# Attention into a two-layer expert on one Trainium2 core: fewer loads of x, three of seven low weight parts from DRAM, two sets of weight sums, the expert's load queue in written order

## The chip, the cores and the metric

The kernel runs on one core of a Trainium2 chip. It is one launch, and the metric is the device time of that launch in microseconds (us). The core has five engines that run side by side and meet at semaphores: TensorE (PE) multiplies into PSUM, VectorE (DVE) and ScalarE (ACT) read PSUM and SBUF, GpSimd (POOL) works on SBUF alone, and SyncE (SP) issues nearly all transfers here. Each engine takes its instructions strictly in the order in which they stand in its queue.

## The reference, cut to what matters

```
scores = q k^T / 8 + bias          # 4 batches x 8 heads x 576 x 576, heads of 64
attn   = exp(scores - max) / (sum + 1e-9)
x      = attn v, heads side by side           # 2304 tokens x 512
h = x @ w_in                                  # 512 -> 2048
g = h where h >= 1, 0 where h <= -1, else (h + 1)**2 / 4
out = g @ w_out                               # 2048 -> 512, float32
```

The bias is a small two-layer network of the distance of two positions.

## The kernel before

Every float32 operand of a product is split into a high part (a rounded copy) and a low part (the value minus its high part), and a product is three matmuls: high by high, high by low, low by high.

The program has three parts. The bias network comes first (to 72 us) and goes to DRAM. Attention follows (to about 324 us): 16 units of one batch and two heads each. Each unit's result is stored to `xT` in DRAM as values that are not yet divided, in a high and a low half, and the reciprocals of the sums of exponentials go to `rT`. The expert is the rest, over three blocks of 768 tokens (`TB`), each cut into two halves of 384 (`TH`).

Loading x for a block is eight loads (`load_x`), each of one row group k of 128 and one half j of the tokens: two transfers bring the two heads' rows, and several more bring the reciprocals, each spread over 64 partitions. The reciprocals' row in `rT` has the first 512 of both heads ahead of the last 64 of both, so a load is cut at 512 too. DVE then adds the two halves (L393) and multiplies by the reciprocal (L394).

Block 0 (324 to 453 us) multiplies plainly, in 32 steps `m` (16 slices of 128 rows f of the hidden layer, two halves). The same steps bring in the 14 weight slices of each layer that are still missing: `job(m, 0)` loads raw values, ACT and DVE put them in order, POOL makes the low part (L143), and the second layer's slices, once split, are stored to `w2d` (`job(m - 2, 6)`). The steps also prepare x of block 1.

Blocks 1 and 2 (from 453 us) share one loop with 16 groups g, eight in each block. A group is two slices f of the hidden layer by both halves, and by Winograd's form of Strassen's scheme it takes seven products instead of eight, steps `s_` 0 to 6; `t` counts steps through all groups. Steps 0, 2 and 5 multiply by a quarter of the first layer's weights as it is; steps 1, 3, 4 and 6 multiply by a sum of quarters. There are four such sums in four tiles `S_`, which DVE forms (L816, `sum_s`) one group ahead: sums 0 to 2 of group g + 1 at steps 1 to 3 of group g, and the last sum of g at its step 1. For each step the high part is made on ACT four steps ahead (L825, `high_w`) and the low part three steps ahead (L835, `low_w`), on DVE for step 1 and on POOL for the other six. So in each group POOL makes six low parts of weights and four low parts `gl` of the activations (L921).

The result of each step lands in one of two PSUM banks (`h_bank`), taken in turn. DVE combines it (L928) with what earlier steps left; until it has, PE can't begin the step after next. Four results of a group pass on: ACT squares (L913, L914), DVE clamps (L919), ACT makes `gh` (L920), POOL makes `gl`. Between the products, `chunks` runs the second layer's matmuls on the activations of the group before, 12 chunks in a group. The second layer's weights come back from `w2d` (L947).

Block 2's x is prepared inside the loop of block 1 (`make_x`): a table says at which step each load is issued and after how many steps DVE adds and multiplies; DVE forms four further matrices of differences (L768, `combine_x`), and `part_x` makes the high part on ACT (L774) and the low part on POOL (L775).

What sets the order: on PE, ACT, DVE and POOL the order of this part is that of the written program (`keep`). SP's queue was not held so: a scheduler placed the transfers.

Of the kernel before, what the change touches and what calls it, by code (L numbers as in the profile page):

```python
# [62 lines left out]
def attn_cpb_moe_kernel(ctx, tc, qk, vL, cb, win, wout, lw, ident, ii, out):  # L63
# [12 lines left out]
    rT = [[dram.tile([2 * S], F32, name=f"rT{p}_{b}") for b in range(B)] for p in range(NP)]  # L76
# [35 lines left out]
    def weight_ahead(f, o, rp):  # L112
# [32 lines left out]
        def store():  # L145
            if o:
                nc.sync.dma_start(out=w2d[f], in_=both[f].bitcast(F32))
# [4 lines left out]
    go = [False]  # L152

# [211 lines left out]
    def load_x(blk, k, j, home="x"):  # L365

        src = xT[k][blk // TB][:, :, TH * j : TH * j + TH].rearrange("(s d) i c -> d s i c", s=2)
# [10 lines left out]
        for i in range(2):  # L378
            nc.sync.dma_start(out=r[D * i : D * i + D], in_=src[:, :, i])
        c0 = blk + TH * j  # L380
        c1 = c0
        while c1 < c0 + TH:
            t = c1 % S
            e = min(c0 + TH, c1 - t + (512 if t < 512 else S))
            for i in range(2):
                at = 512 * i + t if t < 512 else 1024 + D * i + t - 512
                row = rT[k][c1 // S][at : at + e - c1].unsqueeze(0)
                nc.sync.dma_start(out=rr[D * i : D * i + D, c1 - c0 : e - c0], in_=row.to_broadcast((D, e - c1)))
            c1 = e
        return r, rr  # L390

    def scale_x(r, rr, out):
        keep(nc.vector.tensor_tensor(out=r[:, 0], in0=r[:, 0], in1=r[:, 1], op=ALU.add))  # L393
        keep(nc.vector.tensor_tensor(out=out, in0=r[:, 0], in1=rr, op=ALU.mult))  # L394
# [20 lines left out]
    with ExitStack() as ph:  # L415
# [39 lines left out]
        def unit(n):  # L455
# [124 lines left out]
            def store(half):  # L580
# [83 lines left out]
    with ExitStack() as ph:  # L664
# [12 lines left out]
        pinned = [False]  # L677

# [21 lines left out]
        def chunks(n_):  # L700
            for _ in range(n_):
# [12 lines left out]
                if last:  # L714
                    o = gp.tile([P, DM], F32, tag="o", name=f"o{blk}_{at_}", bufs=CFG["ob"])
                    r = blk + P * at_
                    if blk == 2 * TB and not made and len(prev) == 1 and t == TH // P - 1:
# [4 lines left out]
                        nc.sync.dma_start(out=out[r : r + P, h_:], in_=o[:, h_:])  # L722
                    else:
# [4 lines left out]
                        nc.sync.dma_start(out=out[r : r + P, :], in_=o)  # L728
                prev[0][-1] += 1
                if t == TH // P - 1:  # L730
                    prev.pop(0)

# [22 lines left out]
        def fill_x(blk, q):  # L755
            k, j, o, i = NEXT[q]
            r = load_x(blk, k, j, "x" if q % 2 else "y")

            def scale():
                stage[o, i] = room_b(q)  # L760
                scale_x(*r, stage[o, i])

            return scale
# [7 lines left out]
        def part_x(blk, o, k):  # L771
            h, l = xo[blk][o][k]
            x = stage[o, k]
            keep(nc.scalar.copy(h, x))  # L774
            keep(nc.gpsimd.tensor_tensor(out=l, in0=x, in1=h.bitcast(F32), op=ALU.subtract))  # L775
# [33 lines left out]
        def sum_s(g, which):  # L809
            if g >= 2 * NG2:  # L810
                return
            f = 2 * (g % NG2)
            (a11, a12), (a21, a22) = [[full[0, f + i][:, c : c + 2 * P] for c in (0, 2 * P)] for i in range(2)]
            for i in which:
                x, y, op = ((a21, a22, ALU.add), (S_[0], a11, ALU.subtract), (a11, a21, ALU.subtract), (a12, S_[1], ALU.subtract))[i]
                keep(nc.vector.tensor_tensor(out=S_[i], in0=x, in1=y, op=op))  # L816

        pair = {}

        def high_w(i):  # L820
# [4 lines left out]
            keep(nc.scalar.copy(pair[i // 2][0][:, half(i)], source(i)))  # L825

# [3 lines left out]
        def low_w(i):  # L830
            if i >= 2 * NW:
# [20 lines left out]
        def make_x(blk, t0, loads_at, wait, todo_at):  # L852
            for o in ("B11", "B21", "B22", "T3", "T1", "T2", "T4"):
                at(t0, room_x, blk, o)
            for q in range(8):
                scales = []
                at(t0 + loads_at[q], lambda q=q, scales=scales: scales.append(fill_x(blk, q)))
                at(t0 + loads_at[q] + wait, lambda scales=scales: scales[0]())
            for k in range(2):
                for i, (o, new) in enumerate(TODO):  # L860
                    if new:
                        at(t0 + todo_at[k][i], combine_x, o, k)
                    at(t0 + todo_at[k][i], part_x, blk, o, k)
# [182 lines left out]
```

## Time and profile before

| what | value |
|---|---|
| median of three runs | 726.49 us (726.26 to 729.02) |
| the profiled execution, whole | 727.38 us |
| its span, first to last instruction | 725.6 us |
| PE busy | 688.8 us, 95% of the span |
| DVE, ACT, POOL busy | 575.9, 522.9, 522.9 us |

The profile is of one execution, and its instructions carry times from the start of the span. A busy PE is not a PE at its peak, since matmuls overlap and their ends are modelled; the start times of equal matmuls are the sounder measure. An engine's busy share over the span is an average over parts that are bound by different things, so the parts are read one by one.

### The profile page before, as it was taken

How to read it: one execution, taken by the hardware profiler on the slowest of the kernel's cores; microseconds unless marked ns; L12 is line 12 of the kernel's file. 1: busy time of each engine (PE TensorE's matmuls, PEld its weight loads, DVE VectorE, ACT ScalarE, POOL GpSimd, SP SyncE). 2: the span in 40 equal slices, each digit the busy share in tenths (PEclk: the TensorE clock that was granted, in tenths of full speed). 3: DMA queues.
4: the chain of work that ended last, by engine and by line, in shares of the span. 5: the costliest groups of instructions: out<-in, count | busy, mean ns of one | idle time of the engine just before them, and what ended most of it. 6: DMA issues, size and time to landing. Idle time of an engine off the chain costs nothing. (4 is left out here: it accounts for less than half of the span.)

```text
span 725.6 us, 14168 instructions
## 1 busy us (share of the span) xinstructions
PE 688.8 (95%) x4816; PEld 593.4 (82%) x4816; DVE 575.9 (79%) x1061; ACT 522.9 (72%) x1166; POOL 522.9 (72%) x480
## 2 busy tenths in 40 slices
PE   5776999999999999999999999998999999999997
PEld 2233799989897899889999999887878888888986
DVE  7998888889899989987999988568876667655543
ACT  8897899999997898885556665455566556665553
POOL 7985678888888898874678998456777745555542
PEclk9898999999999999999999999999999999999999
DMA  6689625545743653435788782454312224122123
GB/s 225 216 265 284 203 94 193 164 149 163 230 129 111 191 139 124 130 109 181 239 255 248 224 241 87 161 164 141 109 58 60 59 76 157 59 75 71 59 64 112
DMA packets 58153, 109.16 MB, mean 150 GB/s; under 512 B 11985, under 2 KB 32225, under 8 KB 58081
## 3 DMA queue, kind: packets, MB, share of 16 engines
q1 hardware_dynamic: 57792, 108.04, 48.2%
q8 instruction: 38, 0.62, 0.4%
q14 instruction: 35, 0.28, 0.1%
q10 hardware_dynamic: 288, 0.22, 0.1%
HBM read 74.72 MB, written 33.51 MB: 149 GB/s over the span
## 5 line engine op out<-in xcount | busy, mean ns | idle before, releaser
L680 PE MATMUL y<-w,gh 128*128 128x512 f32 x576 | 180.2, 393 | 0.0
L921 POOL TENSOR_TENSOR gl<-c,gh 128x384 fp32r<-128x384 f32 x64 | 66.9, 1046 | 96.5 <-ACT gh L920 40.9
L680 PEld LDWEIGHTS y<-w,gh 128*128 128x128 f32 x576 | 106.7, 189 | 13.3
L680 PE MATMUL y<-w,gl 128*128 128x512 f32 x288 | 114.1, 396 | 0.0
L463 ACT ACTIVATE e<-e,mx 128x576 f32<-128x576 f32 x128 | 99.2, 776 | 17.2 <-DVE mx L466 16.3
L466 DVE CUSTOM_DVE_ANT_0 e<-S,bias 128x576 f32<-128x576 f32 x128 | 92.2, 748 | 13.9 <-PE S L440 13.8
L551 POOL TENSOR_TENSOR lo<-c,hi 128x512 fp32r<-128x512 f32 x64 | 83.4, 1304 | 5.1
L919 DVE SCALAR_TENSOR_TENSOR c<-h,c 128x384 f32<-128x384 f32 x64 | 50.0, 781 | 43.5 <-ACT c L914 38.1
L550 POOL CAST hi<-c 128x512 fp32r<-128x512 f32 x64 | 43.4, 678 | 42.2 <-ACT c L542 42.2
L913 ACT ACTIVATE c<-h,half_s 128x384 f32<-128x384 f32 x64 | 39.5, 618 | 47.3 <-DVE h L928 46.5
L443 PE MATMUL T<-id_s,e 128*128 128x128 f32 x512 | 73.5, 277 | 0.1
L920 ACT CAST gh<-c 128x384 fp32r<-128x384 f32 x64 | 32.9, 514 | 42.9 <-DVE c L919 37.9
L680 PEld LDWEIGHTS y<-w,gl 128*128 128x128 f32 x288 | 54.3, 188 | 11.6
L443 PEld LDWEIGHTS T<-id_s,e 128*128 128x128 f32 x512 | 59.6, 143 | 4.5 <-ACT e L463 2.3
L281 ACT ACTIVATE u<-lw,nthr 128x576 f16<-128x576 f32 (+17 forms) x104 | 57.5, 643 | 4.4 <-DVE lw L246 2.4
L300 PEld LDWEIGHTS <-qh 128*32 128x32 f16 x704 | 19.2, 103 | 48.2 <-issue 21.2
L895 POOL TENSOR_TENSOR gl<-c,gh 128x384 fp32r<-128x384 f32 x32 | 37.2, 1163 | 29.7 <-ACT gh L892 16.5
L283 POOL TENSOR_SCALAR u<-lw,thr 128x576 f16<-128x576 f32 (+17 forms) x36 | 51.7, 1450 | 7.8 <-DVE lw L246 3.9
L440 PE MATMUL O<-hi,vs 128*128 128x256 f32 (+1 forms) x320 | 57.0, 308 | 0.2 <-POOL xl L411 0.2
L440 PE MATMUL O<-lo,vs 128*128 128x256 f32 (+1 forms) x320 | 55.3, 303 | 0.0
L158 POOL TENSOR_TENSOR ls<-qk,kh 128x640 fp32r<-128x640 f32 x32 | 54.0, 1709 | 0.0
L440 PE MATMUL S<-kh 64*128 64x288 f32 x256 | 49.1, 349 | 4.4 <-DVE mx L466 3.4
(186 smaller groups left out, 1999.9 us busy)
## 6 DMA issues: line engine op xcount, KB each, us to landing
w<-w2d SPq DMA_DIRECT2D x32, 512.0 KB, 3.5
bias_d<-y SPq DMA_DIRECT2D x36, 295.5 KB, 4.4
qk<-in_qk_dram SPq DMA_DIRECT2D x16, 640.0 KB, 4.8
x<-xT SPq DMA_DIRECT2D x48, 192.0 KB, 3.9
raw<-in_win_dram SPq DMA_DIRECT2D x16, 512.0 KB, 4.5
raw<-in_wout_dram SPq DMA_DIRECT2D x16, 512.0 KB, 5.2
w2d<-w SPq DMA_DIRECT2D x16, 512.0 KB, 2.8
v<-in_vL_dram SPq DMA_DIRECT2D x16, 320.0 KB, 3.0
```

What stands on the lines that cost most here:

```text
L158: pool(nc.gpsimd.tensor_tensor(out=o, in0=i, in1=h.bitcast(F32), op=ALU.subtract))
L281: tc.keep_in_program_order(nc.scalar.activation(u[:, :n_], lw1[:, :n_], AF.Sigmoid, bias=nthr[:, m : m + 1], scale=STEEP))
L283: EN[x].tensor_scalar(out=u[:, :n_], in0=lw1[:, :n_], scalar1=thr[:, m : m + 1], scalar2=None, op0=ALU.is_gt)
L440: keep(nc.tensor.matmul(*a, **k))
L443: keep(nc.tensor.transpose(*a))
L463: keep(nc.scalar.activation(ev, ev, AF.Exp, bias=m, scale=-1.0, accum_out=sm[:, at : at + 1]))
L466: keep(nc.vector.tensor_tensor_reduce(out=o.rearrange("p (a b) -> p a b", a=2), in0=ps[:, :, :HS], in1=of.rearrange("p (a b) -> p a b", a= ...
L550: keep(nc.gpsimd.tensor_copy(hi, ps))
L551: keep(nc.gpsimd.tensor_tensor(out=lo, in0=ps, in1=hi.bitcast(F32), op=ALU.subtract))
L680: a = nc.tensor.matmul(out, w, x, start=start, stop=stop)
L919: keep(nc.vector.scalar_tensor_tensor(out=c, in0=h, scalar=1.0, in1=c, op0=ALU.max, op1=ALU.min))
L921: keep(nc.gpsimd.tensor_tensor(out=gl, in0=c, in1=gh.bitcast(F32), op=ALU.subtract))
```

## The change

What it does, part by part:

1. **x in DRAM.** A unit's result is stored in the layout in which it is loaded: two stores of 64 partitions each in place of one of 128. A load of x is one transfer of 128 partitions in place of two of 64. The reciprocals are stored as two plain rows, by two transfers in place of one, and are loaded with cuts at 576 alone.
2. **Low parts from DRAM.** In block 0 the low parts of the quarters that steps 0, 2 and 5 use are stored to a new `w1d`, 256 KB or 128 KB from each of 16 slices. In blocks 1 and 2 `high_w` issues a load of 128 KB for each of these steps, four steps ahead, and `low_w` leaves them out: 48 loads in place of 48 subtractions on POOL.
3. **Two sets of sums.** `S_` has eight tiles; groups take them in turn.
4. **x of block 2.** Loads at every fourth step (0 to 29) instead of every third; the add and the multiplication now stand one step apart; what follows starts 3 and 7 steps later; the low parts are made on DVE, a step after the high parts, 14 of them. For block 1's x the low parts stay on POOL.
5. **SP in written order.** From block 0 on the transfers pass through `dma`, which holds them in written order. Stores of `w2d` and `w1d` are written one step later (`job(m - 3, 6)`), and stores of the output are held back until two younger ones wait (`ready`, `flush`).

```diff
-            nc.sync.dma_start(out=w["raw"].rearrange("p a b -> p (a b)"), in_=src.bitcast(I32))
+            dma(out=w["raw"].rearrange("p a b -> p (a b)"), in_=src.bitcast(I32))
...
             if o:
-                nc.sync.dma_start(out=w2d[f], in_=both[f].bitcast(F32))
+                dma(out=w2d[f], in_=both[f].bitcast(F32))
+            else:
+                c = DM // 2 * (f % 2)
+                dma(out=w1d[f][:, c:], in_=parts[0, f][1][:, c:].bitcast(F32))
...
+    def dma(**kw):
+        ins = nc.sync.dma_start(**kw)
+        if queued[0]:
+            keep(ins)
...
-        for i in range(2):
-            nc.sync.dma_start(out=r[D * i : D * i + D], in_=src[:, :, i])
+        dma(out=r, in_=src)
...
-            e = min(c0 + TH, c1 - t + (512 if t < 512 else S))
+            e = min(c0 + TH, c1 - t + S)
...
-                nc.sync.dma_start(out=rT[p][b].rearrange("(k q) -> k q", q=P), in_=r)
+                nc.sync.dma_start(out=rT[p][b][:, :512].rearrange("j (k q) -> j k q", q=P), in_=r[:8])
+                nc.sync.dma_start(out=rT[p][b][:, 512:], in_=r[8:9])
...
-                    nc.sync.dma_start(out=xT[p][c1 // TB][:, :, c1 % TB : c1 % TB + e_ - c1], in_=x[:, :, c1 - c0 : e_ - c0])
+                    dst = xT[p][c1 // TB][:, :, c1 % TB : c1 % TB + e_ - c1].rearrange("(i d) s c -> s d i c", i=2)
+                    for s_ in range(2):
+                        dma(out=dst[s_], in_=x[D * s_ : D * s_ + D, :, c1 - c0 : e_ - c0])
...
-                        nc.sync.dma_start(out=out[r : r + P, h_:], in_=o[:, h_:])
+                        dma(out=out[r : r + P, h_:], in_=o[:, h_:])
...
-                        nc.sync.dma_start(out=out[r : r + P, :], in_=o)
+                        ready.append((out[r : r + P, :], o))
+                        if len(ready) > 2:
+                            flush()
...
-            keep(nc.gpsimd.tensor_tensor(out=l, in0=x, in1=h.bitcast(F32), op=ALU.subtract))
+            en = nc.vector if blk > TB else nc.gpsimd
+            keep(en.tensor_tensor(out=l, in0=stage[o, k], in1=h.bitcast(F32), op=ALU.subtract))
...
-                return S_[{4: 0, 1: 1, 3: 2, 6: 3}[s_]]
+                return S_[i // NS % 2][{4: 0, 1: 1, 3: 2, 6: 3}[s_]]
...
             keep(nc.scalar.copy(pair[i // 2][0][:, half(i)], source(i)))
+            if i % NS in (0, 2, 5):
+                f = i % NW // NS * 2 + (i % NS == 5)
+                c = 2 * P * (i % NS > 0)
+                dma(out=pair[i // 2][1][:, half(i)].bitcast(F32), in_=w1d[f][:, c : c + 2 * P])
...
-            if i >= 2 * NW:
+            if i >= 2 * NW or i % NS in (0, 2, 5):
                 return
...
-        make_x(2 * TB, 0, (1, 4, 7, 10, 13, 16, 19, 22), 4, (range(16, 35, 3), range(28, 47, 3)))
+        make_x(2 * TB, 0, range(1, 30, 4), 4, (range(19, 38, 3), range(35, 54, 3)))
...
-            job(m - 2, 6)
+            job(m - 3, 6)
...
         for i in ORDER[:4]:
             prev.append(made.pop(i))
             chunks(3)
+            while ready:
+                flush()
```

On PE nothing moves. On POOL, around steps 1 and 2 of group 4 in block 1 (weights `w_8` and `w_9`), there stood before, with `T2l` and `B11l` low parts of block 2's x, `w0l` of weights and `gl` of activations:

```order
L921 TENSOR_TENSOR gl_6_1_7933<-c_6_1_7910,gh_6_1_7932 128x384
L775 TENSOR_TENSOR T2l_1536_7164<-b_7482,T2h_1536_7163 128x384
L775 TENSOR_TENSOR B11l_7150<-b_7645,B11h_7149 128x384
L835 TENSOR_TENSOR w0l_7928<-sum_w_5776,w0h_7927 128x256
L835 TENSOR_TENSOR w0l_7928<-w_9_5762,w0h_7927 128x256
L835 TENSOR_TENSOR w0l_7975<-sum_w_5779,w0h_7974 128x256
L921 TENSOR_TENSOR gl_8_0_8001<-c_8_0_7979,gh_8_0_8000 128x384
```

and now:

```order
L952 TENSOR_TENSOR gl_6_1_7957<-c_6_1_7934,gh_6_1_7956 128x384
L863 TENSOR_TENSOR w0l_7952<-sum_w_5834,w0h_7951 128x256
L863 TENSOR_TENSOR w0l_8001<-sum_w_5837,w0h_8000 128x256
L952 TENSOR_TENSOR gl_8_0_8030<-c_8_0_8005,gh_8_0_8029 128x384
```

Three of seven are gone from POOL there. On DVE, at the same place, there stood before (the second `sum_w` is sum 0 of the next group, into the tile that POOL's first `w0l` above reads):

```order
L768 TENSOR_TENSOR b_7482<-b_7482,b_7312 128x384
L928 TENSOR_TENSOR u_7959<-p_1_7942,p_1_7930 128x384
L816 TENSOR_TENSOR sum_w_5779<-w_8_5761,sum_w_5777 128x256
L816 TENSOR_TENSOR sum_w_5776<-w_11_5764 128x256
L928 TENSOR_TENSOR h_2_7977<-p_2_7963,p_1_7930 128x384
L816 TENSOR_TENSOR sum_w_5777<-sum_w_5776,w_10_5763 128x256
```

and now, where `sum_v` is the second set, L778 the add of a load of x, L782 its multiplication, and L798 a low part of x:

```order
L959 TENSOR_TENSOR u_7980<-p_1_7962,p_1_7954 128x384
L840 TENSOR_TENSOR sum_w_5837<-w_8_5819,sum_w_5835 128x256
L840 TENSOR_TENSOR sum_v_7184<-w_11_5822 128x256
L778 TENSOR_TENSOR x_3_1_7879<-x_3_1_7879 128x384
L798 TENSOR_TENSOR B22h_7215<-b_7604,B22h_7215 128x384
L959 TENSOR_TENSOR h_2_8003<-p_2_7990,p_1_7954 128x384
L840 TENSOR_TENSOR sum_v_7185<-sum_v_7184,w_10_5821 128x256
L782 TENSOR_TENSOR b_8009<-x_3_1_7879 128x384
```

Sum 0 of the next group goes to another tile than the one POOL reads, and an add and a low part now stand ahead of `h_2`, which frees PE's bank. On SP, the last transfers were before:

```order
L728 DMA out_dram<-o_0_9907 128x512
L728 DMA out_dram<-o_1_9913 128x512
L728 DMA out_dram<-o_2_9919 128x512
L728 DMA out_dram<-o_3_9925 128x512
L728 DMA out_dram<-o_4_9931 128x512
L722 DMA out_dram<-o_5_9937 128x256
```

and are now:

```order
L160 DMA out_dram<-o_0_9943 128x512
L160 DMA out_dram<-o_1_9948 128x512
L160 DMA out_dram<-o_2_9953 128x512
L160 DMA out_dram<-o_5_9971 128x256
L160 DMA out_dram<-o_3_9961 128x512
L160 DMA out_dram<-o_4_9966 128x512
```

The half of `o_5`, which is written last, stands ahead of `o_3` and `o_4`.

## Rows read from the trace of the kernel before

**Rows 1.** Stages: length, busy us (count) by engine, PE clock, DMA share, GB/s.

```profile
core 0: us, PE busy (x) PEld busy (x) DVE busy (x) ACT busy (x) POOL busy (x), PEclk, DMA share, GB/s
324.00:453.20 129.20, 128.91 (x659) 117.58 (x658) 113.27 (x153) 78.04 (x141) 100.22 (x77) 1.00 0.69 212
453.20:619.40 166.20, 161.07 (x782) 141.29 (x781) 117.93 (x191) 97.90 (x216) 105.53 (x114) 0.99 0.35 107
619.40:711.00 91.60, 91.60 (x459) 82.30 (x458) 51.51 (x92) 52.80 (x115) 49.27 (x57) 1.00 0.23 70
```

**Rows 2.** PE's timeline, first product of groups 0, 10, 11, 15: start, length.

```profile
453.19 0.33 PE L680 MATMUL p<-B11h,w0h 128*128 128x384 f32 x1
...
619.36 0.33 PE L680 MATMUL p<-B11h,w0h 128*128 128x384 f32 x1
...
635.01 0.33 PE L680 MATMUL p<-B11h,w0h 128*128 128x384 f32 x1
...
697.60 0.33 PE L680 MATMUL p<-B11h,w0h 128*128 128x384 f32 x1
```

**Rows 3.** PE's timeline, its longest waits: start, length, idle before and releaser.

```profile
479.66 0.44 PE L680 MATMUL p<-T1h,w0h 128*128 128x384 f32 x1 [0.80 <-DVE h L928]
...
501.70 0.41 PE L680 MATMUL p<-B22h,w0h 128*128 128x384 f32 x1 [1.89 <-DVE u L928]
...
531.85 0.44 PE L680 MATMUL p<-T1h,w0h 128*128 128x384 f32 x1 [1.16 <-DVE h L928]
```

**Rows 4.** Stage table for the stretch at the lower clock, columns as in Rows 1.

```profile
502.20:505.60 3.40, 3.40 (x11) 2.91 (x10) 2.32 (x5) 2.98 (x8) 1.51 (x2) 0.50 0.53 162
```

**Rows 5.** DVE's timeline ahead of the PE wait that ends at 531.85.

```profile
530.39 0.93 DVE L816 TENSOR_TENSOR sum_w<-w 128x256 f32<-128x256 f32 x1 [2.58 <-POOL w0l L835]
531.25 0.54 DVE L928 TENSOR_TENSOR h<-p,p 128x384 f32<-128x384 f32 x1
```

**Rows 6.** POOL's timeline over the same time.

```profile
528.65 1.01 POOL L775 TENSOR_TENSOR B11l<-b,B11h 128x384 fp32r<-128x384 f32 x1
529.63 0.73 POOL L835 TENSOR_TENSOR w0l<-sum_w,w0h 128x256 fp32r<-128x256 f32 x1
```

**Rows 7.** Waits of the whole span: waiter, releaser, us in total, times, longest.

```profile
DVE sum_w L816 <- POOL w0l L835: 16.4, 14, 2.6
...
ACT x L578 <- DMA xT<-x: 1.9, 1, 1.9
```

**Rows 8.** Costliest groups, whole span: POOL's low parts of plain weights.

```profile
L835 POOL TENSOR_TENSOR w0l<-w,w0h 128x256 fp32r<-128x256 f32 x48 | 39.0, 812 | 0.0
```

**Rows 9.** DVE's timeline, adds and multiplications of x: beside an idle and a busy POOL.

```profile
490.94 0.54 DVE L393 TENSOR_TENSOR x<-x 128x384 f32<-128x384 f32 x1
...
498.25 1.09 DVE L393 TENSOR_TENSOR x<-x 128x384 f32<-128x384 f32 x1
499.38 1.25 DVE L394 TENSOR_TENSOR b<-x 128x384 f32<-128x384 f32 x1
```

**Rows 10.** Groups by line, 453.2 to 571 us: DVE on block 2's x (us, mean ns).

```profile
L394 DVE TENSOR_TENSOR b<-x 128x384 f32<-128x384 f32 x8 | 7.8, 978 | 0.3
L393 DVE TENSOR_TENSOR x<-x 128x384 f32<-128x384 f32 x8 | 7.4, 922 | 0.0
...
L768 DVE TENSOR_TENSOR b<-b,b 128x384 f32<-128x384 f32 x8 | 5.6, 706 | 0.0
```

**Rows 11.** DMA issues: KB each, median us to landing.

```profile
w<-w2d SPq DMA_DIRECT2D x32, 512.0 KB, 3.5
```

**Rows 12.** SP's issues of xT: ns min/median/max.

```profile
L586 SPq DMA_DIRECT2D xT<-x x40: 519/557/1513, 88.8 to 328.1; - x40
```

**Rows 13.** PE's timeline, last high product of steps m = 6 and 30 in block 0.

```profile
346.13 0.33 PE L680 MATMUL h<-xh,w0h 128*128 128x384 f32 x1
...
446.43 0.33 PE L680 MATMUL h<-xh,w0h 128*128 128x384 f32 x1
```

**Rows 14.** SP's timeline at the end: the last issue.

```profile
722.61 0.33 SPq L722 DMA_DIRECT2D out_dram<-o  x1
```

**Rows 15.** SP's other issues of output: ns min/median/max.

```profile
L728 SPq DMA_DIRECT2D out_dram<-o x17: 332/338/1119, 463.2 to 721.7; - x17
```

**Rows 16.** GB/s moved from 716 to 727 us, in 40 slices of 0.275 us.

```profile
GB/s 0 0 0 0 0 0 0 0 0 0 0 0 0 74 410 380 373 380 365 417 365 380 380 365 372 417 309 343 339 52 0 0 0 0 0 0 0 0 0 0
```

More of the change, by code (lines that the diff above doesn't have):

```diff
@@ L75, in attn_cpb_moe_kernel @@
     w2d = [dram.tile([P, 2 * DM], F32, name=f"w2d{f}") for f in range(DFF // P)]
-    rT = [[dram.tile([2 * S], F32, name=f"rT{p}_{b}") for b in range(B)] for p in range(NP)]
+    w1d = [dram.tile([P, DM], F32, name=f"w1d{f}") for f in range(DFF // P)]
+    rT = [[dram.tile([2, S], F32, name=f"rT{p}_{b}") for b in range(B)] for p in range(NP)]
     NF = DFF // P
@@ L383, in load_x @@
             t = c1 % S
-            e = min(c0 + TH, c1 - t + (512 if t < 512 else S))
+            e = min(c0 + TH, c1 - t + S)
             for i in range(2):
-                at = 512 * i + t if t < 512 else 1024 + D * i + t - 512
-                row = rT[k][c1 // S][at : at + e - c1].unsqueeze(0)
-                nc.sync.dma_start(out=rr[D * i : D * i + D, c1 - c0 : e - c0], in_=row.to_broadcast((D, e - c1)))
+                row = rT[k][c1 // S][i : i + 1, t : t + e - c1].to_broadcast((D, e - c1))
+                dma(out=rr[D * i : D * i + D, c1 - c0 : e - c0], in_=row)
             c1 = e
         return r, rr
-    def scale_x(r, rr, out):
-        keep(nc.vector.tensor_tensor(out=r[:, 0], in0=r[:, 0], in1=r[:, 1], op=ALU.add))
-        keep(nc.vector.tensor_tensor(out=out, in0=r[:, 0], in1=rr, op=ALU.mult))
     def split_x(k, j, home):
@@ L731, in chunks, with flush @@
                     prev.pop(0)
+        ready = []
+        def flush():
+            to, o = ready.pop(0)
+            dma(out=to, in_=o)
         def g_tiles(blk, f, j):
@@ L757, in fill_x, with add @@
             r = load_x(blk, k, j, "x" if q % 2 else "y")
+            x, rr = r[0][:, 0], r[1]
+            def add():
+                keep(nc.vector.tensor_tensor(out=x, in0=x, in1=r[0][:, 1], op=ALU.add))
             def scale():
                 stage[o, i] = room_b(q)
-                scale_x(*r, stage[o, i])
-            return scale
+                keep(nc.vector.tensor_tensor(out=stage[o, i], in0=x, in1=rr, op=ALU.mult))
+            return add, scale
         def combine_x(o, k):
@@ L812, in sum_s @@
             f = 2 * (g % NG2)
+            sw = S_[g % 2]
             (a11, a12), (a21, a22) = [[full[0, f + i][:, c : c + 2 * P] for c in (0, 2 * P)] for i in range(2)]
             for i in which:
-                x, y, op = ((a21, a22, ALU.add), (S_[0], a11, ALU.subtract), (a11, a21, ALU.subtract), (a12, S_[1], ALU.subtract))[i]
-                keep(nc.vector.tensor_tensor(out=S_[i], in0=x, in1=y, op=op))
+                x, y, op = ((a21, a22, ALU.add), (sw[0], a11, ALU.subtract), (a11, a21, ALU.subtract), (a12, sw[1], ALU.subtract))[i]
+                keep(nc.vector.tensor_tensor(out=sw[i], in0=x, in1=y, op=op))
         pair = {}
@@ L856, in make_x @@
                 scales = []
-                at(t0 + loads_at[q], lambda q=q, scales=scales: scales.append(fill_x(blk, q)))
-                at(t0 + loads_at[q] + wait, lambda scales=scales: scales[0]())
+                at(t0 + loads_at[q], lambda q=q, scales=scales: scales.extend(fill_x(blk, q)))
+                for i in range(2):
+                    at(t0 + loads_at[q] + wait + i, lambda i=i, scales=scales: scales[i]())
             for k in range(2):
@@ L862, in make_x @@
                         at(t0 + todo_at[k][i], combine_x, o, k)
-                    at(t0 + todo_at[k][i], part_x, blk, o, k)
+                    at(t0 + todo_at[k][i], high_x, blk, o, k)
+                    at(t0 + todo_at[k][i] + (blk > TB), low_x, blk, o, k)
         make_x(TB, T0, (1, 3, 5, 7, 9, 11, 13, 15), 2, (range(10, 23, 2), range(17, 30, 2)))
-        make_x(2 * TB, 0, (1, 4, 7, 10, 13, 16, 19, 22), 4, (range(16, 35, 3), range(28, 47, 3)))
-        S_ = [bx.tile([P, 2 * P], F32, name=f"sum_w{i}") for i in range(4)]
+        make_x(2 * TB, 0, range(1, 30, 4), 4, (range(19, 38, 3), range(35, 54, 3)))
+        S_ = [[bx.tile([P, 2 * P], F32, name=f"sum_w{i}") for i in range(4)]]
         at(-4, sum_s, 0, (0, 1, 2))
@@ L901, in attn_cpb_moe_kernel @@
             due(T0 + m)
-        job(2 * NF - 2, 6)
-        job(2 * NF - 1, 6)
+        for m in range(2 * NF - 3, 2 * NF):
+            job(m, 6)
         raws.close()
         um = ph.enter_context(tc.tile_pool(name="m_u", bufs=1))
+        S_.append([um.tile([P, 2 * P], F32, name=f"sum_v{i}") for i in range(4)])
         pinned[0] = True
@@ L946, in attn_cpb_moe_kernel @@
                     parts[1, fo] = ring(1, i)
-                    nc.sync.dma_start(out=both[i].bitcast(F32), in_=w2d[fo])
+                    dma(out=both[i].bitcast(F32), in_=w2d[fo])
                 if open_act and s_ > 3:
```

13 lines of the change are left out of this document (9 added, 4 removed).

## The prediction

> **What bounds the kernel now.** I read the stages first. In block 0 and in most of blocks 1 and 2 PE is busy nearly all the time; between 453 and 619 us it stands still for 5 us, and DVE and POOL work there for 118 and 106 of 166 us [rows 1]. A busy PE can hide lost time, so I go by starts of equal matmuls. From the first product of group 11 to that of group 15 it is 62.59 us for four groups, 15.65 us each; from group 0 to group 10 it is 166.17 us, where ten groups at 15.65 are 156.5 [rows 2]. So **9.7 us are lost** between 453 and 619 us, and hardly any later: group 10 too takes 15.65.
>
> Where do they go? PE's longest waits there are 0.80, 1.89 and 1.16 us, all for DVE to free a PSUM bank [rows 3]. After the one of 1.89 us PE's granted clock is 0.50, the lower of its levels, 1.2 GHz, for 3.4 us, in which 1.7 us of full pace are lost [rows 4]. Shorter waits and refilling the array make up the rest, which shows in the starts alone. Now follow the wait that ends at 531.85 back: DVE does `h` at 531.25, because a `sum_w` ahead of it waited 2.58 us for POOL [rows 5]; POOL got to that low part only at 529.63, behind two low parts of x, of which the later took 1.01 us [rows 6]. DVE wants to overwrite a tile of sums that POOL hasn't read yet. Over the span this is 16.4 us in 14 waits [rows 7].
>
> **The change, part by part.**
>
> *Two sets of sums.* The next group's sum 0 goes to a tile that POOL read a whole group earlier. The 14 waits go, and what is late next on DVE is its own work.
>
> *Low parts from DRAM.* POOL loses 48 subtractions of 812 ns, 39.0 us in all [rows 8], three of ten in each group. Since POOL has idle time in blocks 1 and 2, this alone saves nothing; it takes POOL out of the chain. What comes in its place is 48 loads of 128 KB. A load is written four steps ahead of its use, some 8.9 us at 15.65 us for seven steps, and its slot was freed a step earlier still. A 512 KB load of the same kind lands 3.5 us after issue [rows 11]. About 5 us are spare, so I take the loads at nothing; a load that comes later than that costs PE the difference.
>
> *Low parts of x on DVE.* This is a new cost on the engine that PE waits for. The nearest rows are DVE's adds and multiplications of x: 0.54 us beside an idle POOL, 1.09 and more where POOL works [rows 9]; the 24 such steps that DVE does now take 20.8 us, 0.87 each [rows 10]. I take 0.87 for each of 14, 12.2 us (bounds 0.54 and 1.09: 7.6 and 15.3). The work on block 2's x then spreads over 54 steps, 7.7 groups, 120.7 us at full pace. DVE's steady work there is 51.51 us in 91.6 [rows 1], 8.8 a group, 67.9 in 7.7 groups. With 20.8 and 12.2 that is 101 us, **84%** (80 to 86%). In block 0 DVE is busy 113.27 of 129.2 us, 88% [rows 1], and PE keeps an even 4.18 us a step there: 100.30 us for 24 steps [rows 13]. So 84% can be carried if it comes evenly. It does so better than before, since add and multiplication stand apart. I leave **1.0 us** of stalls, one of the size of the first or third in [rows 3]; the bounds are 0 and 0.8 in each of seven groups, 5.6 us.
>
> *Rule and row.* The row of 0.54 against that of 1.09 shows that DVE's steps with two inputs in SBUF run long beside POOL. The Trainium skill (SBUF — State Buffer, Who interferes with whom) says more: a DVE instruction with two SBUF inputs and a GpSimd instruction that reads SBUF can't run together, and the later one stands fully blocked until the earlier ends. The trace agrees as far as the doubling goes. By that rule this part of the change is a mistake if the low parts meet POOL each time, and the time would be that of the first rival below.
>
> *Loads and stores of x, SP's order.* A load of x is one transfer in place of two, and four to two of reciprocals in place of six to two. That frees SP time. Against it stand 40 more stores of `xT`, at 0.557 us of SP each [rows 12], 22 us over some 240 us of attention, and 16 more of `rT`. Engines wait for such a store once, ACT for 1.9 us at the end of attention [rows 7], where it would wait for DVE anyway. No engine's order moves in attention. I take it at nothing, with 1 us to either side.
>
> *Block 0.* 3.1 MB more are stored there, 24 GB/s beside 212 [rows 1]. PE loses nothing now, so nothing can be won. The stores written a step later stand less in front of the raw loads. I take nothing, with a loss of up to 1 us in the bound.
>
> *The end.* Here the change costs something plain. SP's last issue is now the half of `o_5`, at 722.61 [rows 14], with `o_3` and `o_4` issued before it. After the change these two come behind it, 0.34 us each and a small gap [rows 15], together 0.76. The last store is also 256 KB and not 128, 0.35 us more at some 375 GB/s [rows 16]. I take **1.0 us** (0.7 to 1.5).
>
> **The sum.** The profiled execution took 727.38 us. Less 9.7, plus 1.0 for stalls that stay and 1.0 at the end, it is 719.7. The median of the three runs is 0.9 below the profiled one, so I predict **718.8 us**. The bounds of the terms give 717.5 to 723.9; with 1 us for attention I say 716.5 to 724.5.
>
> **The rivals.**
>
> *DVE becomes the bound.* The wait of 1.89 us had no wait for POOL directly ahead of it: DVE added and multiplied x there for 2.34 us at a stretch [rows 9], at POOL's pace. If the 14 low parts and the longer x work do this in each group, 5.6 us stay instead of 1.0: **723.4 us**. Against it speaks that POOL's work from 453 to 619 us falls from 63% to some 42% (30 of its 0.81 us and 14 of about 1.0 go), so that DVE meets it less often.
>
> *The traffic of block 0.* The stretch moves 212 GB/s at a DMA share of 0.69 already [rows 1]. If the stores push 28 raw loads late by 0.3 us each, ACT and then PE follow, 8.4 us: **727 us**, no difference. Against it: the raw loads go out earlier than before.
>
> *Loads that come late, the case that ends slower.* SP now works strictly in written order, so one transfer that waits holds all behind it. The place is a load of x whose tile DVE hasn't read yet, with low parts behind it. It decides from the point where SP is held longer than the 5 us spare; then steps 0, 2 and 5 wait for their weights. If each of 16 groups lost 1 us so, it would be 718.8 + 16 = **735 us**. The gain is used up at 0.16 us on each of the 48 loads. Against it: an x tile is free three steps before its load is written, and output stores wait for two younger ones.
>
> *The change doesn't do what it says*: DVE could be held by something other than the tile of sums. That is the first rival's case in its strongest form, and the rows of 531 us name POOL too plainly for a chance of its own.
>
> **How the numbers follow.** 0.71 for the forecast, 0.14 for DVE as the bound, 0.07 each for traffic and late loads. What a measurement of this kernel can tell from no change is about 0.5%, 3.6 us: faster is below 722.9, slower above 730.1. Faster takes the forecast and half of DVE's case, 0.78; no difference takes the rest of it and the traffic, 0.14; slower 0.08. The range of 716.5 to 724.5 holds the first two cases but for their edges, about 0.8.
>
> **What would show it.** Group starts after 453 us at 15.65 us each, from the first; no wait of DVE `sum` for POOL; the granted clock at its upper level from 453 us on; POOL's low parts of plain weights gone; the first product of group 15 some 9 us earlier against the start of group 0; the last output transfers about 1 us later against PE's last matmul. I am wrong on DVE if PE still waits for `h` or `u` between 460 and 575 us with DVE busy without a gap, wrong on the loads if PE waits for a DMA, and wrong on block 0 if its steps are longer than 4.18 us.

## The result, and the profile of the changed kernel

The changed kernel takes **721.35 us** (median of five runs, 719.13 to 722.13); the kernel before, run beside it, took 727.48 (726.26 to 729.15). The ratio is 0.989, with a 95% interval of 0.987 to 0.992: faster by some 1.1%. 718.8 us had been predicted, with a range of 716.5 to 724.5. The profiled execution of the changed kernel took 721.35 us, its span 719.6.

The first thing to read is the timeline of PE, as in [rows 2]: the first product of groups 0, 10, 11 and 15 (start, length).

```profile
454.56 0.33 PE L688 MATMUL p<-B11h,w0h 128*128 128x384 f32 x1
...
611.97 0.33 PE L688 MATMUL p<-B11h,w0h 128*128 128x384 f32 x1
...
627.62 0.33 PE L688 MATMUL p<-B11h,w0h 128*128 128x384 f32 x1
...
690.20 0.33 PE L688 MATMUL p<-B11h,w0h 128*128 128x384 f32 x1
```

Ten groups from group 0 to group 10 take 157.41 us where they took 166.17; against 156.5 at full pace, 0.9 us are lost instead of 9.7. From group 0 to group 15 it is 235.64 us against 244.41, a gain of **8.8 us**. The stage table answers to [rows 1] (length, busy us and count by engine, PE clock, DMA share, GB/s): block 0, the stretch that lost time, and the rest.

```profile
326.00:454.50 128.50, 128.43 (x656) 117.53 (x657) 101.11 (x152) 78.57 (x140) 95.52 (x75) 1.00 0.72 231
454.56:611.97 157.41, 157.29 (x781) 140.77 (x780) 109.03 (x206) 98.19 (x217) 64.65 (x69) 1.00 0.48 146
611.97:703.00 91.03, 91.03 (x456) 81.82 (x455) 46.84 (x91) 52.15 (x113) 36.21 (x41) 1.00 0.30 93
```

PE stands idle for 0.1 us in the middle row, where it stood for 5, and its granted clock is 1.00 throughout. POOL works 65 us there, not 106. Block 0 moves 231 GB/s instead of 212.

Of 8.8 us, 6.0 reach the profiled time. The other two pieces lie at the two ends. Group 0 starts at 454.56, not 453.19, 1.4 us later. And from the first of the last output copies (710.82) to the end of the span it is 8.8 us, where it was 7.4 (718.22 to 725.6), again 1.4. So 727.38 - 8.8 + 1.4 + 1.4 = 721.4. The end first: GB/s moved from 709 to 720 us in 40 slices of 0.275 us, as in [rows 16].

```profile
GB/s 0 0 0 0 0 0 0 0 0 0 0 0 276 365 373 380 387 395 372 313 0 0 0 0 290 268 339 220 380 410 395 365 194 0 0 0 0 0 0 0
```

And SP's timeline, its last six issues as one row (start, length):

```profile
711.54 4.99 SPq L160 DMA_DIRECT2D out_dram<-o  x6
```

Four empty slices, 1.1 us, stand between the first three stores and the last ones. The copies of `o_3` and `o_4` are done by then, but SP waits for the half of `o_5`, which stands ahead of them; in [rows 16] there is no gap.

The start is another matter. Attention's stage tables, 225 to 235 us, before and after:

```profile
225.00:235.00 10.00, 8.77 (x78) 7.64 (x79) 9.34 (x19) 8.53 (x23) 6.82 (x8) 1.00 0.40 124
```

```profile
225.00:235.00 10.00, 8.76 (x66) 7.52 (x62) 7.78 (x16) 7.36 (x21) 6.81 (x7) 0.83 0.57 156
```

PE's busy time is the same, with fewer instructions. A row of the changed kernel inside the second table shows why:

```profile
230.20:233.60 3.40, 3.40 (x18) 3.07 (x16) 2.36 (x6) 3.10 (x9) 0.62 (x2) 0.50 0.83 205
```

For 3.4 us the granted clock is 0.50, 1.2 GHz, which costs 1.7 us of full pace. Block 0's first product then starts at 328.89 instead of 327.39. What PE does ahead of the fall is no different from before. Around its wait of 0.95 us for DVE there, in the changed kernel up to the fall and at the same place in the kernel before:

```profile
225.20:230.20 5.00, 3.76 (x33) 3.12 (x32) 4.84 (x10) 3.82 (x11) 4.67 (x5) 1.00 0.43 131
```

```profile
225.89:230.89 5.00, 3.77 (x32) 3.13 (x32) 4.84 (x10) 3.81 (x11) 4.68 (x5) 1.00 0.39 131
```

All runs below but the first leave attention as it is in the changed kernel. Two of their eleven profiles have such a stretch too (another order of the last stores, a dose of DVE work), with block 0 at 328.8 and 329.1; the other nine have none, and block 0 starts at 326.0 to 327.5. So it comes in some executions and not in others, and the change isn't shown to bring it. The five times of the changed kernel lie at 719.1 to 719.2, with a mean granted clock of 0.992 to 0.994, and at 721.4 to 722.1, with 0.987 to 0.990. The two groups are about such a stretch apart; as only one execution was profiled, that this is the reason is argued, not shown. One execution among the runs below, 843.25 us at a mean granted clock of 0.751, is left out of its kernel's figures.

On DVE, 54 steps from group 0 on (groups by line: us, mean ns of one):

```profile
L778 DVE TENSOR_TENSOR x<-x 128x384 f32<-128x384 f32 x8 | 5.5, 683 | 0.0
...
L782 DVE TENSOR_TENSOR b<-x 128x384 f32<-128x384 f32 x8 | 4.4, 547 | 0.0
L798 DVE TENSOR_TENSOR B11l<-b,B11h 128x384 fp32r<-128x384 f32 x2 | 1.6, 820 | 0.0
L798 DVE TENSOR_TENSOR B22l<-b,B22l 128x384 fp32r<-128x384 f32 x1 | 1.4, 1372 | 0.0
...
L798 DVE TENSOR_TENSOR T2l<-b,T2h 128x384 fp32r<-128x384 f32 x2 | 1.1, 546 | 0.0
```

The multiplications went from 978 to 547 ns and the adds from 922 to 683 [rows 10]. The low parts of x, 13 in this stretch, are 8.4 us, 0.65 each.

### The profile page after: what moved, and what is told of

Read it like the earlier page. It is cut to its first block, busy times and chain, and to the rows that moved or that the text cites. A ratio compares the mean times of both kernels' runs of the same rounds, so it can differ in the third digit from the quotient of the medians.

```text
span 719.6 us, 14291 instructions
## 1 busy us (share of the span) xinstructions
PE 685.9 (95%) x4816; PEld 595.0 (83%) x4816; DVE 550.7 (77%) x1075; ACT 524.3 (73%) x1166; POOL 464.9 (65%) x418
## 4 chain that ended last, share of the span: by engine, by line
PE 78%; DVE 7%; ACT 2%; DMA 2%; issue 1%; SPq 1%; ACTq 0%; DVEq 0%
PE y L688 27%; PE p L688 16%; PE h L688 9%; PE O L444 9%; PE S L444 7%; PE T L447 6%; DVE e L470 2%; PE T_s L447 1%; PE S_L L444 1%; DVE lo L557 1%; DVE x L406 1%; PE T_L L447 1%; DVE sum L560 1%; ACT e L467 1%; DVE x L409 1%
## 5 line engine op out<-in xcount | busy, mean ns | idle before, releaser
L950 DVE SCALAR_TENSOR_TENSOR c<-h,c 128x384 f32<-128x384 f32 x64 | 42.3, 662 | 42.3 <-ACT c L945 28.1
```

The source lines that it names most:

```text
L950: keep(nc.vector.scalar_tensor_tensor(out=c, in0=h, scalar=1.0, in1=c, op0=ALU.max, op1=ALU.min))
```

## Experiments

All rest on one number, the **loss**: the time from group 0 to group 10 less 156.5 us. It was 9.7 before and is 0.9 after. It is read in one profiled execution of each kernel; five of these, the changed kernel among them, give 0.90 to 0.94. Theory A is the prediction's: sums wait for POOL to read their tile, and PE waits for DVE behind them. Theory C grew from its first rival (each expectation says what the letters in it stand for): what PE waits for is a lump of DVE work on x that stands ahead of `h` and `u`.

**Two sets of sums alone**, in the kernel before.

```diff
-                return S_[{4: 0, 1: 1, 3: 2, 6: 3}[s_]]
+                return S_[i // NS % 2][{4: 0, 1: 1, 3: 2, 6: 3}[s_]]
```

> The kernel before with two sets of weight sums and nothing else of the change. Theory A (DVE waits to overwrite a tile of sums that POOL has not read): the waits of DVE's sums for POOL go (16.4 us before), and of the 9.7 us lost from group 0 to group 10 only stalls from DVE's own work stay, such as the one of 1.89 us with its stretch at the lower clock, 3 to 4 us; gain about 6 us on the kernel before. Theory B (POOL's sheer amount of work holds DVE back, by the slower steps beside it, not by the tile): loss stays at 8 us or more, gain under 2 us.

722.41 us, ratio 0.993 (0.991 to 0.995). The sums' waits for POOL are gone from the table of waits, all 16.4 us of [rows 7], yet the loss is 5.7 us, and PE still waits. DVE's timeline ahead of its longest wait, and PE's row (start, length, idle before and releaser):

```profile
494.00 1.24 DVE L817 TENSOR_TENSOR sum_v<-w,w 128x256 f32<-128x256 f32 x1
495.17 1.09 DVE L393 TENSOR_TENSOR x<-x 128x384 f32<-128x384 f32 x1
496.29 1.25 DVE L394 TENSOR_TENSOR b<-x 128x384 f32<-128x384 f32 x1
497.46 0.55 DVE L930 TENSOR_TENSOR h<-p,p 128x384 f32<-128x384 f32 x1
497.93 0.54 DVE L930 TENSOR_TENSOR u<-p,u 128x384 f32<-128x384 f32 x1
...
498.62 0.41 PE L680 MATMUL p<-B22h,w0h 128*128 128x384 f32 x1 [1.20 <-DVE u L930]
```

A sum, the add and the multiplication stand one behind the other, each at some two to three times its short price (0.41 and 0.54 us elsewhere), and hold `h` and `u` back. Nothing waits for a tile of sums. The loss is 4.0 us smaller, between the two expectations. Some 1.7 us of that are the stretch at half clock [rows 4], which this execution doesn't have, so theory A holds for 2.3 to 4.0 of the 8.8 us.

**The changed kernel with one set of sums.**

```diff
-                return S_[i // NS % 2][{4: 0, 1: 1, 3: 2, 6: 3}[s_]]
+                return S_[0][{4: 0, 1: 1, 3: 2, 6: 3}[s_]]
```

> The changed kernel with one set of sums in place of two; POOL is still relieved of three of six low parts of weights and of the low parts of x. Theory A: waits of DVE's sums for POOL come back in each group, but short, since POOL has less ahead of the low part that is waited for; loss from group 0 to 10 between 1 and 4 us, 0 to 3 us slower than the changed kernel. Theory B: loss as in the changed kernel, 0.9 us, and the same time.

719.33 us, ratio 0.990 (0.987 to 0.992), loss 0.9. The waits are back, 5.1 us in 5, and PE loses nothing by them, where theory A expected 1 to 4 us. With the rest of the change in place the second set isn't needed.

**Low parts of block 2's x on POOL again.**

```diff
-            en = nc.vector if blk > TB else nc.gpsimd
+            en = nc.gpsimd
```

> The changed kernel with the 14 low parts of block 2's x on POOL again. If the prediction's sum for DVE is right (84% of the time with them, which can be carried), taking them off DVE changes nothing that is bound: loss from group 0 to 10 stays within 0.5 us of 0.9 us, same time within 1 us. If DVE as the bound was a near thing, the 0.9 us go and the time falls by up to 1 us. If POOL still matters, the loss rises above 2 us.

718.77 us, ratio 0.989 (0.986 to 0.992), loss 0.9. Nor is this part needed by itself. The stage tables over 120 us from group 0 on, of the changed kernel and of this one, show something better:

```profile
454.56:574.56 120.00, 119.94 (x597) 107.56 (x596) 85.79 (x161) 75.05 (x166) 49.93 (x54) 1.00 0.49 149
```

```profile
451.87:571.87 120.00, 119.94 (x597) 107.56 (x596) 85.30 (x148) 75.23 (x166) 64.77 (x67) 1.00 0.49 149
```

DVE does 13 instructions fewer in the second and is busy for the same time, 85.30 against 85.79 us. What it saves it gives back beside a busier POOL: its clamps `c` take 22.0 us there (757 ns each) and 19.7 (680) in the changed kernel, the sums 20.5 and 18.1, the low parts of weights 4.6 and 2.9.

**The changed kernel with the old table of x**, one set and low parts on POOL: the loads of low parts, the new layout in DRAM and SP's written order are left.

```diff
-                    at(t0 + loads_at[q] + wait + i, lambda i=i, scales=scales: scales[i]())
+                    at(t0 + loads_at[q] + wait, lambda i=i, scales=scales: scales[i]())
...
-        make_x(2 * TB, 0, range(1, 30, 4), 4, (range(19, 38, 3), range(35, 54, 3)))
+        make_x(2 * TB, 0, (1, 4, 7, 10, 13, 16, 19, 22), 4, (range(16, 35, 3), range(28, 47, 3)))
```

> The changed kernel with one set of sums, the low parts of block 2's x on POOL, and the old table for block 2's x (loads every third step, add and multiplication together). What stays of the change in blocks 1 and 2 is the low parts from DRAM and the order of SP's queue. Theory A (POOL comes late to the low part that DVE's sum waits for, because of all that stands ahead of it): taking three of six low parts of weights off POOL is enough, loss from group 0 to 10 at most 2.5 us of 9.7. Rival theory C (DVE's own lumps of work on x make the stalls, and the new table evens them out): loss 3 us or more, with PE waiting for DVE at the places of an add and a multiplication.

724.49 us (five runs of 722.38 to 726.09), ratio 0.996 (0.994 to 0.998). The loss is read in a second run of the same kernel.

> The kernel with the low parts from DRAM and the order of SP's queue, but one set of sums, the low parts of block 2's x on POOL and the old table for block 2's x, once more, for the profile. It took 722.4 to 726.1 us, 3 to 5 us more than with the new table. Theory A alone (POOL late to the low part that a sum waits for): loss from group 0 to 10 at most 2.5 us, and the time is lost elsewhere (before 450 us or at the end). Theory C beside it (DVE's lumps of work on x): loss of 3 to 6 us, in waits of PE for DVE where an add and a multiplication stand together.

723.84 us, ratio 0.995 (0.993 to 0.997), loss 5.5. Sums wait 12.6 us in 8, PE waits 1.8 us for `h` and 0.5 for `u`. This is in theory C's range, but theory A's chain can be seen once more; DVE's rows, then PE's:

```profile
526.99 0.93 DVE L840 TENSOR_TENSOR sum_w<-w 128x256 f32<-128x256 f32 x1 [2.58 <-POOL w0l L863]
527.84 0.55 DVE L958 TENSOR_TENSOR h<-p,p 128x384 f32<-128x384 f32 x1
...
528.45 0.44 PE L688 MATMUL p<-T1h,w0h 128*128 128x384 f32 x1 [1.35 <-DVE h L958]
```

**The changed kernel without the loads**, with one set: POOL makes all low parts of weights again.

```diff
-            if i % NS in (0, 2, 5):
-                f = i % NW // NS * 2 + (i % NS == 5)
-                c = 2 * P * (i % NS > 0)
-                dma(out=pair[i // 2][1][:, half(i)].bitcast(F32), in_=w1d[f][:, c : c + 2 * P])
...
-            if i >= 2 * NW or i % NS in (0, 2, 5):
+            if i >= 2 * NW:
```

> The changed kernel with one set of sums and without the low parts from DRAM (no stores to w1d, no loads, all six low parts of weights on POOL or DVE as before). What stays is the new table for block 2's x, its low parts on DVE, and the order of SP's queue. Theory A: POOL loses 14 low parts of x of 1.0 us but keeps 48 of weights; waits of DVE's sums for POOL stay at 8 us or more, loss from group 0 to 10 between 2 and 5 us. Theory C: loss at most 1.5 us.

721.48 us, ratio 0.993 (0.991 to 0.996), loss 3.2, waits of sums 12.7 us in 14. Here theory A's range holds (2 to 5 us) and theory C's bound of 1.5 doesn't. PE's longest wait has both behind it, a sum that waited for POOL and then an add at its long price:

```profile
522.41 0.93 DVE L837 TENSOR_TENSOR sum_w<-w 128x256 f32<-128x256 f32 x1 [1.60 <-POOL w0l L856]
523.27 1.09 DVE L775 TENSOR_TENSOR x<-x 128x384 f32<-128x384 f32 x1
524.28 0.55 DVE L795 TENSOR_TENSOR B22h<-b,B22h 128x384 fp32r<-128x384 f32 x1
524.75 0.55 DVE L951 TENSOR_TENSOR h<-p,p 128x384 f32<-128x384 f32 x1
...
525.35 0.44 PE L685 MATMUL p<-T1h,w0h 128*128 128x384 f32 x1 [0.58 <-DVE h L951]
```

**Only the loads and the new table of x**: one set, low parts on POOL, SP's order left to the scheduler.

> This is the changed kernel with one set of sums, with the low parts of block 2's x on POOL again and with SP's transfers placed by the scheduler; what stays of the change is the layout and spacing of the loads of x, the add and the multiplication a step apart, and the low parts of weights from DRAM. Theory C (DVE held PE up with lumps of x work, and POOL was too full; the loads and the new table of x mend it, the rest is not needed): ten groups from group 0 to group 10 take 157.2 to 157.8 us, PE has no wait for DVE from 453 to 619 us, sums wait for POOL for 5 to 8 us in all without harm, the last group's start to the end of the span is 28.0 us, and the time is 717.5 to 719.5 us. Theory A (the tile of sums is what matters, and a set of its own or a POOL without x must free it): with neither of the two, DVE's sums wait for POOL some 12 us and more as with the old table, ten groups take 160 us or more, and the time is 721 us or more.

718.29 us, ratio 0.989 (0.985 to 0.992), loss 1.5, from the last group's start to the end 28.0 us. The table of waits holds both halves of the answer (waiter, releaser, us, times, longest):

```profile
PE p L688 <- DVE h L958: 0.3, 1, 0.3
...
DVE sum_w L840 <- POOL w0l L863: 12.5, 9, 2.6
```

Sums wait as long as with the old table, 12.5 us against 12.6, and the loss is 1.5 instead of 5.5. The waits themselves cost little once x is spread out. The longest of them is as long as the one ahead of 531.85 in the kernel before [rows 5], but PE has no wait behind it, and its group takes 15.79 us:

```profile
538.35 1.23 DVE L840 TENSOR_TENSOR sum_w<-w 128x256 f32<-128x256 f32 x1 [2.58 <-POOL w0l L863]
539.50 0.55 DVE L958 TENSOR_TENSOR h<-p,p 128x384 f32<-128x384 f32 x1
```

POOL is as busy in both (63 of 120 us), yet DVE's multiplications of x take 549 ns with the new table and 962 with the old one: the table also sets whether they meet POOL's work. The run is nearer to theory C than to A: it lies within C's range in time, but it lost 0.2 us more than C allowed, has one wait of PE for DVE (0.3 us) where C had none, and its sums wait as long as A had said. Side by side:

| x table | loads | sets | low parts of x | sums wait for POOL, us | loss, us |
|---|---|---|---|---|---|
| old | no | 1 | POOL | 16.4 | 9.7 (before) |
| old | no | 2 | POOL | 0 | 5.7 |
| old | yes | 1 | POOL | 12.6 | 5.5 |
| new | no | 1 | DVE | 12.7 | 3.2 |
| new | yes | 1 | POOL | 12.5 | 1.5 |
| new | yes | 1 | DVE | 5.1 | 0.9 |
| new | yes | 2 | POOL | 0 | 0.9 |
| new | yes | 2 | DVE | 0 | 0.9 (after) |

The 9.7 holds the stretch at half clock; without its 1.7 us it is 8.0. The loads, the new table and the second set each go with over 2 us less in a kernel that lacks the other two, and what each is worth depends on which of the others are there. Rows three, four and six to eight have SP in written order, the others don't; the last run of this section shows no loss by that. The new table has several pieces (loads further apart, add and multiplication a step apart, later differences), which no run takes apart, and no run undoes the new layout in DRAM by itself.

**A dose of DVE work**: each low part of block 2's x made three times.

```diff
-            keep(en.tensor_tensor(out=l, in0=stage[o, k], in1=h.bitcast(F32), op=ALU.subtract))
+            for _ in range(3 if blk > TB else 1):
+                keep(en.tensor_tensor(out=l, in0=stage[o, k], in1=h.bitcast(F32), op=ALU.subtract))
```

> The changed kernel with each of the 14 low parts of block 2's x on DVE made three times, 28 more steps on DVE. In the changed kernel DVE is busy 86 of 120.8 us over the 54 steps in which block 2's x is prepared, a low part takes 0.65 us on average; with 28 more it is 104 us, 86%. If the prediction's sum holds (88% can be carried), the loss from group 0 to 10 rises by less than 1.5 us over 0.9. If DVE as the bound was near, by 3 us or more.

726.29 us, ratio 0.999 (0.997 to 1.001), loss 8.2: with 28 subtractions more nothing of the gain in the groups is left but 1.5 us. PE waits 5.0 us in 6 for `h` and `u`. DVE's timeline with a lump, and PE's wait behind it:

```profile
543.46 2.14 DVE L799 TENSOR_TENSOR B11l<-b,B11h 128x384 fp32r<-128x384 f32 x3
545.51 0.55 DVE L960 TENSOR_TENSOR h<-p,p 128x384 f32<-128x384 f32 x1
...
546.12 0.44 PE L688 MATMUL p<-T1h,w0h 128*128 128x384 f32 x1 [0.55 <-DVE h L960]
```

The stage table, columns as above:

```profile
453.00:573.00 120.00, 114.71 (x561) 100.18 (x560) 94.72 (x172) 69.03 (x153) 47.61 (x49) 1.00 0.48 142
```

DVE is busy 79% here and holds PE up; in block 0 it was 88% busy and didn't [rows 1, 13]. An average share doesn't say what an engine can carry. Three subtractions at once are a lump, though; the run doesn't say what 79% in single steps would do.

**Loads of weights two steps ahead of their use, and one step**, instead of four.

```diff
+                load_w(t + 2)
```

> The changed kernel with each load of a low part written two steps ahead of its use in place of four (4.5 us in place of 8.9). The prediction took a load at 3.5 us from issue to landing and 5 us as spare: so nothing is lost or up to 0.3 us in a few of 48 loads, within 1.5 us of the changed kernel, a few waits of PE for DMA. The rival of late loads: if SP's queue holds loads back by more than 1 us, each of the 48 loads stalls PE, 10 us or more slower.

719.24 us, ratio 0.990 (0.988 to 0.991), loss 1.3. The 0.4 us more lie in group 1, where a weight load on PE waits 0.4 us for its low part.

> The changed kernel with each load of a low part written one step ahead of its use (2.2 us in place of 8.9). If a load takes about 2 to 3.5 us from issue to landing, as taken in the prediction, it is late by some 0.5 to 1.5 us, and PE stalls at up to 48 steps: 15 to 60 us slower than the changed kernel, with PE waiting for DMA at steps 0, 2 and 5. If the loads land within one step, no difference.

At one step ahead 727.74 us, ratio 1.000 (0.998 to 1.002). The profiled execution, 724.51 us, is the fastest of eight (to 729.69); its loss is 6.9, with PE's rows:

```profile
471.63 0.44 PE L688 MATMUL p<-B11h,w0l 128*128 128x384 f32 x1 [2.81 <-DMA w0l<-w1d]
...
599.73 0.44 PE L688 MATMUL p<-B11h,w0l 128*128 128x384 f32 x1 [1.46 <-DMA w0l<-w1d]
```

Four waits, 5.6 us in all, where stalls at up to 48 steps had been expected: 44 loads come in time even so. The four late ones lie in the first two groups of blocks 1 and 2, where SP also stores the output of the block before. SP's rows ahead of the wait of 2.81 us:

```profile
467.39 1.00 SPq L160 DMA_DIRECT2D out_dram<-o  x2
468.44 0.96 SPq L160 DMA_DIRECT2D w0l<-w1d  x2
```

The load is issued only at 468.44, behind these stores, when the step that uses it has begun. For these four the edge lies between 4.5 and 2.2 us ahead of use. PE's clock didn't fall behind the wait of 2.81 us, though it had behind that of 1.89 us in the kernel before [rows 4]:

```profile
471.60:476.00 4.40, 4.37 (x21) 3.91 (x22) 1.95 (x4) 1.55 (x5) 2.51 (x4) 1.00 0.98 324
```

**The end.** First the held-back stores let go ahead of the last one, then SP's order left to the scheduler.

```diff
+                        while ready:
+                            flush()
                         nc.scalar.dma_start(out=out[r : r + P, :h_], in_=o[:, :h_])
```

> The changed kernel with the last stores in the old order (o_3 and o_4 ahead of the half of o_5). The end after the first output copy, 8.78 us in the changed kernel and 7.38 us before, goes back to 7.4 us; 1.2 to 1.4 us faster than the changed kernel. If the end were longer for another reason, no difference.

718.43 us, ratio 0.988 (0.986 to 0.990); from the last group's start to the end 28.0 us, not 29.4, as in the kernel before.

```diff
-        queued[0] = True
+        queued[0] = False
```

> The changed kernel with SP's queue placed by the scheduler again (not held in written order). If written order only keeps things as they are, same time within 1 us and loss from group 0 to 10 of 0.9 us. If it is needed for the loads of low parts to come in time, PE waits for DMA and the loss rises by 2 us or more.

717.74 us, ratio 0.988 (0.986 to 0.990), 28.0 us again, loss 0.9. GB/s at its end, from 706 to 717 us, have no gap:

```profile
GB/s 0 0 0 0 0 0 0 0 0 0 0 0 0 0 0 112 395 365 373 380 395 387 372 380 372 365 387 402 309 347 328 52 0 0 0 0 0 0 0 0
```

So the place of two held-back stores behind the half of `o_5` costs 1.4 us; written order as such costs nothing here (the first of the two runs keeps it) and brings nothing that these runs show. Both medians lie below both kernels'. How much below the changed kernel is less sure, since the stretch at half clock in attention moves its medians too; the 1.4 us at the end is read inside single profiles.

## Why the prediction was right, and where it was not

*What is lost: 9.7 us.* Right. The starts of equal matmuls gave the size, and 8.8 of it came back, where 9.7 less 1.0 had been put. PE's idle time alone, 5 us, would have said too little. Of the 9.7, 1.7 us are the stretch at half clock behind the wait of 1.89 us. That the wait brings it isn't shown, since a wait of 2.81 us has none behind it, and no second profile of the kernel before says whether it comes each time.

*Why it is lost.* Half right, and this is the step that failed. The prediction followed the wait at 531.85 back to POOL [rows 5, 6] and then let that one chain stand for all of the loss. With that chain gone the loss is still 5.7 us. The other wait, 1.89 us at 501.70 [rows 3], with adds and multiplications ahead of it [rows 9], is the same lump that stays in the run with two sets alone; the first rival had named it. That rival's mechanism came true for the two sets alone. That its 5.6 us lie so near the 5.7 measured is chance: it reckoned 0.8 us in seven groups for the whole change, with low parts on DVE that this run doesn't have. For the whole change it did not come true: with the new table and the loads PE has no wait for DVE.

*Low parts from DRAM: "this alone saves nothing; it takes POOL out of the chain".* Too little. With the old table the loads, with the new layout and SP's order, take 4.2 us off the loss (2.5 but for the stretch at half clock), and with the new one the loads alone take 2.3 (3.2 to 0.9). That they cost nothing four steps ahead is right: two steps would nearly do.

*Low parts of x on DVE: 12.2 us, DVE at 84%.* Mis-sized: 0.65 us each and not 0.87, and DVE is busy 86.17 of 120.8 us, 71%:

```profile
454.50:575.30 120.80, 120.74 (x601) 108.24 (x601) 86.17 (x162) 75.05 (x166) 50.58 (x54) 1.00 0.49 150
```

Of the 15 us less than the 101 reckoned, 4 are the low parts, 6 the adds, multiplications and differences of x (14.6 us in place of 20.8), and 5 DVE's steady work. The price came from rows beside a busy POOL, while the change both takes work from POOL and puts DVE's steps at other places; the prediction used the first against a rival, but neither in its own price. The net cost to DVE is about 0.5 us, as the run with low parts on POOL shows. The Trainium skill (SBUF — State Buffer, Who interferes with whom) would have one of two instructions that meet, a DVE one with two SBUF inputs and a GpSimd one that reads SBUF, stand blocked; the runs agree as far as the price hangs on the meeting, 962 against 549 ns beside a POOL equally busy. That the low parts on DVE would therefore be a mistake isn't borne out: the run without them has the same loss.

*That 84% can be carried, as 88% in block 0.* It was not put to the test, since DVE came to 71%. The share it was argued from says little: at 79%, in lumps, PE loses 8.2 us, though the prediction had asked for work that comes evenly.

*1.0 us of stalls that stay.* The size is right, 0.9, the cause not. PE's table has no wait for DVE there. The 0.9 us are two longer groups at the starts of blocks 1 and 2 (16.00 and 15.94 us) and 0.03 us in each other one, and the kernel before had these two as well (15.99 and 15.96).

*Block 0 at nothing.* Right: the last high product of steps 6 and 30 [rows 13] is 100.16 us apart, against 100.30.

```profile
347.64 0.33 PE L688 MATMUL h<-xh,w0h 128*128 128x384 f32 x1
...
447.80 0.33 PE L688 MATMUL h<-xh,w0h 128*128 128x384 f32 x1
```

*Attention at 0, with 1 us to either side.* 1.4 us later in the profiled pair, from a stretch at half clock that comes and goes.

*The end: +1.0 (0.7 to 1.5).* Right in cause, and 1.4 measured, near the upper bound. The place of the two held-back stores makes it, as the two runs on the end show.

*Late loads.* The rival was real but its cover is thick enough: between two steps ahead and one, four loads come late behind output stores (not behind a load of x, where the prediction looked), and they cost 6.0 of the 8.8 us; the median is then that of the kernel before.

The median is 2.5 us above the forecast. In the profiled execution the sum was 719.7 and 721.35 came, 1.7 more: 1.4 from attention, 0.4 from the end, and 0.1 less from the groups. The other 0.9 is the step to the median, which was taken off and here isn't there.

## What to carry to other kernels

Follow every long wait back before one of them is made the cause of the whole loss: here two mechanisms held PE's banks, and a cure for one left 5.7 of 9.7 us. What an engine could carry here was decided by what stands directly ahead of the instruction that is waited for, not by its busy share, so split long work on the side into single instructions between them. Price a moved instruction at the pace of the kernel after the change, and hold no store behind one that is written earlier but ready later.

## What the runs showed of the hardware

Work between two engines that slow each other was moved here for much less than its own length. The 13 subtractions of 0.65 us, 8.4 us in all, made DVE busier by 0.5 us in 120 with two sets of sums, and by 2.8 us with one set (83.98 against 81.20 us, in two runs whose SP order differs too). DVE's clamps were the faster for it: 680 ns, against 757 while POOL made the low parts at 1.0 to 1.2 us each.

A change of granted clock to 0.50 for 3.4 us shows up in attention in three of the thirteen profiles read here. What PE does ahead of it is the same in all thirteen: it waits 0.95 us or so for DVE, and is busy 3.75 to 3.78 of the 5.00 us around that wait, whether the clock falls then or not. The fall moves all that follows by some 2 us (block 0 starts at 328.8 to 329.1 in the three profiles, at 326.0 to 327.5 in the others), as much as many an edit is worth, so two profiles are compared by stretches and not by their ends. What brings it is open; no run tried it.
